# Hash attention before two MLPs: the head outputs' halves moved by DMA and added by GpSimd, the hash products spread over four tiles, and one place in a pair's tiles for every side job

## The chip, the cores and the metric

The kernel runs on one core of a Trainium2 chip. The metric is the device time of one launch in microseconds (us); for the kernel before it is the median of three runs. TensorE, VectorE, ScalarE, GpSimd and SyncE appear in the profile as PE (PEld: its weight loads), DVE, ACT, POOL and SP (SPq: the queue from which SyncE issues DMAs).

## The reference

Inputs q, k and v have the shape (2, 8, 768, 64) in float32; the weights of the MLPs are 64-bit floats.

```
q_bits = einsum('bhsd,dk->bhsk', q, proj) > 0          # 6 bits; k likewise
mask   = q_bucket[:, :, :, None] == k_bucket[:, :, None, :]
scores = where(mask, (q @ k^T) / sqrt(64), -1e9); scores -= max(scores)
attn   = exp(scores); attn = attn / (sum(attn) + 1e-9)
x      = (attn @ v), heads side by side -> (1536, 512)
x      = (silu(x @ w_gate) * (x @ w_val)) @ w_out       # 512 -> 1536 -> 512
out    = layernorm(h * softmax(h)) @ w_out2,  h = x @ w_in2   # 512 -> 1024 -> 512
```

## The kernel before, in words

Every float32 product is made of three products of a faster 32-bit type: a value is cut into a high and a low part, and high x high, high x low and low x high are summed in PSUM.

The attention works on eight **pairs** of heads (pair 0 to 7; 0 to 3 are batch 0). A pair has twelve **tiles** (0 to 11), each of 128 queries of one head against all 768 keys; three tiles make a **quarter** (384 queries of one head), and from pair 1 on the quarters alternate between the two heads, so that both heads' same queries are two quarters in a row, a **half** of the pair. The loop at L722 goes over the 96 tiles and writes all engines' work out by hand (`tc.manual_schedule()`): each engine runs its instructions in exactly the order in which this loop issues them. For tile i an iteration issues the row maxima of tile i (`top`, L491, DVE), the bias and scale made of it (`nm`, L500, DVE), six transposes of the exponentials of tile i-2 (`t`, L531, PE), the scores of tile i+1 (`s`, L480, PE), the high parts (`eh`, L540, ACT) and low parts (`el`, L544, DVE) of the transposes, a third of a quarter's product with v (`av`, L563 and L567, PE), and the exponentials of tile i with their row sums (`e`, L516, ACT). That is the plain work of a tile: on DVE L491, L500 and twice L544.

Beside it run side jobs at fixed tile numbers:
- `split` (L242 and L246, POOL): high and low parts of a later pair's k, q and v, one step a tile (table in `splitting`).
- `turn` (L405, PE; L414 to L424, ACT): six groups of four transposes a pair that turn k and q of a later pair; each is copied out of PSUM by ACT, and DMAs on SP's queue copy rows between partitions (L422, four a head; L425, one a head). The table is `turning`. A turn uses the PSUM bank `pp`, of which there is one.
- `hashes` (L439, PE; L444, DVE): six products of 384 columns in `pp` for each half of the sequence, the bits of which DVE takes out and four small DMAs distribute.
- `sums` and `spread`: 1e-9 is added to a half's row sums (L576, POOL), DVE takes the reciprocal (L578), GpSimd widens it (`wide`, L581, two instructions), three PE transposes bring it to `pp` (L596).
- `results`: a finished `av` holds 64 rows of the product with v's high part and 64 rows of that with its low part. ACT copies the lower 64 rows (`low`, L613), DVE adds them to the upper 64 (L615), once a quarter; once a half DVE multiplies by the spread reciprocals (`xf`, L621), and GpSimd cuts the result into `xh` (L630) and `xl` (L634).
- `early`: twelve DVE steps (L47 to L64) that convert the first 64-bit MLP weights (`w1f`), one after each fourth tile from tile 3 of pair 0 to tile 3 of pair 4 (a DMA takes one of the thirteen places).

`behind` makes a GpSimd instruction wait for the last `nm` that was issued, so that it starts after it. Behind the attention the two MLPs follow; their code is not changed.

Of the kernel before, what the change touches and what calls it, by code (L numbers as in the profile page):

```python
# [20 lines left out]
P = 128  # L21
# [46 lines left out]
def hash_attention_then_two_mlps(  # L68
# [137 lines left out]
    with at:  # L206
# [217 lines left out]
                nc.scalar.copy(qa[:, 1024 - S:S], t)  # L424
                nc.sync.dma_start(qb[0:D].bitcast(F32), qa[0:D].bitcast(F32))  # L425

        def hashes(p, n):
            if p >= len(pairs):
                return
            if n == 0:  # L430
                bits_of[p] = bt.tile([P, S], R32, tag="bits", name="bits")
            cols = slice(HALF * n, HALF * (n + 1))
            t = ps_p.tile([P, 512], F32, tag="pp", name="pp")[:, :HALF]

            for j in range(2):
# [151 lines left out]
        def spread(h):  # L587


            if not 0 <= h < NQ or not ends(h):  # L590
                return
            p, _, n = quarter(h)
# [7 lines left out]
            rs_of[p, n] = rs[:, :HALF]  # L600

        def results(h):
            if not 0 <= h < NQ:
                return
            p, j, n = quarter(h)
# [1 line left out]
            at = slice(j * D, (j + 1) * D)  # L607
            av = av_of.pop(h)
            if j == 0:
                x_of[p, n] = xs.tile([P, HALF], F32, tag="xf", name="xf", bufs=3)  # L610
            xf = x_of[p, n]
# [4 lines left out]
            if not ends(h):  # L616
                return
            del x_of[p, n]
            if p and h < NQ - 1:
                yield  # L620
            nc.vector.tensor_mul(xf, xf, rs_of.pop((p, n)))  # L621
            if h < NQ - 1:
                yield
            cols = slice(b * S + n * HALF, b * S + (n + 1) * HALF)
            if h == NQ - 1:
                nc.scalar.copy(xh[:, hp, cols], xf)
                nc.vector.tensor_sub(xl[:, hp, cols], xf, xh[:, hp, cols].bitcast(F32))
                return
            xh3, xf3 = (x.rearrange("p (c d) -> p c d", d=D) for x in (xh[:, hp, cols], xf))
# [3 lines left out]
            yield  # L633
            behind(nc.gpsimd.tensor_sub(xl[:, hp, cols], xf, xh[:, hp, cols].bitcast(F32)))  # L634

        def go(work):

            next(work, None)

        def turning(p, l):  # L640

            at = {
                0: lambda: turn(p + 1, 0, 1),
                1: lambda: turn(p + 1, 0, 2),
                2: lambda: turn(p + 1, 1, 0),
                3: lambda: turn(p + 1, 1, 1),
                6: lambda: turn(p + 1, 1, 2),
                7: lambda: hashes(p + 1, 0),
                8: lambda: hashes(p + 1, 1),
                9: lambda: turn(p + 2, 0, 0),  # L650
            }
            if p == 1:

                at = {
                    0: lambda: turn(p + 1, 0, 2),
                    2: lambda: turn(p + 1, 1, 0),
                    3: lambda: turn(p + 1, 1, 1),
                    6: lambda: turn(p + 1, 1, 2),
                    7: lambda: hashes(p + 1, 0),
                    8: lambda: hashes(p + 1, 1),  # L660
                    9: lambda: turn(p + 2, 0, 0),
                }
            return at[l]() if l in at else iter(())

        def beginning(i):
# [6 lines left out]
                8: lambda: (hashes(1, 0),),  # L672
                9: lambda: (hashes(1, 1),),
                10: lambda: (turn(2, 0, 0),),
                11: lambda: (turn(2, 0, 1),),
            }
# [19 lines left out]
        def splitting(p, l):  # L696


            if l == 1:
                load(p + 2, "k")  # L700
                load(p + 2, "q")
                load(p + 1, "v")
# [11 lines left out]
        with tc.manual_schedule():  # L714
# [2 lines left out]
            first_weights = early()  # L717
            go(first_weights)
            hashed = start()
            done = summing = leaving = iter(())  # L720
            splits = {}
            for i in range(NSLOT + 9):  # L722
                p, l = divmod(i, SLOTS)
# [5 lines left out]
                if part == 0:  # L729
                    leaving, done = done, results(h - 1)  # L730
                    go(done)
                elif part == 1:
                    go(done)
                maxima(i)
                if part == 0:
                    go(done)
                biases(i)
                transposes(i - 2, 0)
# [8 lines left out]
                for g in range(2):  # L747
                    highs(i - 2, g)
                    lows(i - 2, g)
                if part == 2:  # L750
                    spread(h)
                values(h, part)
                go(work)
                if i == 2:
                    go(hashed)
                if part == 2:
                    go(summing)
# [384 lines left out]
```

## Time and profile before

| | us |
|---|---|
| median of three runs (lowest, highest) | 720.02 (717.36, 720.5) |
| the profiled execution | 719.0 |
| its span, first to last instruction | 717.2 |
| PE busy | 696.4 |
| DVE busy | 567.3 |
| ACT busy | 346.3 |
| POOL busy | 138.3 |

The busy times are sums over the whole span, in which the attention and the MLPs have different limits; they are to be read stage by stage. A matmul's duration includes its way through the array, so PE can be called busy while it is not at its peak.

### The profile page before, as it was taken

To read this page: it belongs to the slowest core of one execution; us is meant where nothing else is said; L and a number is where in the kernel's file an instruction comes from. 1 tells how busy PE (TensorE), PEld (TensorE's weight loads), DVE (VectorE), ACT (ScalarE), POOL (GpSimd) and SP (SyncE) were. 2 spreads that over 40 slices of the span, in tenths; PEclk is the share of its full clock that TensorE was granted. 3 is DMA by queue.
4 is the path that set the end of the run, shared out by engine and by line. 5 is a ranking of instruction groups with operands and counts; after the bars stand their busy time and mean duration, and the time that the engine had idled before them with its cause. 6 is when DMAs were issued, how large, how long until landed. Compare 5 with 4: busy or idle time off the path is not lost.

```text
span 717.2 us, 9973 instructions
## 1 busy us (share of the span) xinstructions
PE 696.4 (97%) x3683; PEld 589.7 (82%) x3683; DVE 567.3 (79%) x988; ACT 346.3 (48%) x676; POOL 138.3 (19%) x157
## 2 busy tenths in 40 slices
PE   8889999999999999999999999999999999999997
PEld 5778898988898887888888888888888888888886
DVE  6899899999889998876797796887987976646461
ACT  6878888888988983343212213122133432222222
POOL 7354345455552314000000000000000000000000
PEclk9999999999999999999999999999999999999999
DMA  6642345260723302322122132232131000000001
GB/s 205 159 116 70 99 121 137 53 165 20 178 60 81 127 1 60 115 85 94 59 75 102 58 118 75 101 90 86 60 118 58 1 0 31 16 29 16 30 15 45
DMA packets 32576, 56.15 MB, mean 78 GB/s; under 512 B 4264, under 2 KB 22952, under 8 KB 32016
## 3 DMA queue, kind: packets, MB, share of 16 engines
q1 hardware_dynamic: 32528, 55.52, 26.5%
q8 instruction: 29, 0.48, 0.3%
q14 instruction: 19, 0.16, 0.1%
HBM read 36.71 MB, written 3.15 MB: 56 GB/s over the span
## 4 chain that ended last, share of the span: by engine, by line
PE 80%; DVE 6%; ACT 5%; DMA 3%; issue 2%; POOL 2%; SPq 0%; ACTq 0%; POOLq 0%
PE h L909 27%; PE h L1022 9%; PE s L480 6%; PE y L935 5%; PE y L934 5%; PE y L936 5%; PE t L531 4%; PE av L563 3%; PE o L1073 3%; PE o L1075 3%; DMA qb<-qa 3%; PE o L1074 3%; PE av L567 2%; ACT eh L540 2%; DVE el L544 2%
## 5 line engine op out<-in xcount | busy, mean ns | idle before, releaser
L909 PE MATMUL h<-xh,lo 128*128 128x512 f32 x288 | 112.3, 390 | 1.1 <-POOL lo L814 1.1
L909 PE MATMUL h<-xh,hi 128*128 128x512 f32 x288 | 112.2, 390 | 0.4 <-ACT hi L813 0.4
L909 PE MATMUL h<-xl,hi 128*128 128x512 f32 x288 | 112.0, 389 | 0.0
L544 DVE TENSOR_TENSOR el<-t,eh 128x384 fp32r<-128x384 f32 x192 | 97.6, 549 | 8.5 <-ACT eh L540 7.7
L516 ACT ACTIVATE e<-s,nm 128x768 f32<-128x768 f32 x96 | 96.8, 1008 | 5.6 <-DVE nm L500 3.0
L491 DVE TENSOR_REDUCE top<-s 128x1 f32<-128x768 f32 x96 | 90.7, 945 | 2.0 <-PE s L480 2.0
L540 ACT CAST eh<-t 128x384 fp32r<-128x384 f32 x192 | 83.6, 487 | 16.7 <-PE t L531 14.9
L1048 POOL TENSOR_TENSOR w<-w,half 128x1 f32<-128x1 f32 x12 | 6.6, 551 | 416.0 <-DVE w L1047 310.8
L531 PE MATMUL t<-idr,e 128*128 128x128 f32 x576 | 81.1, 276 | 0.9 <-DVE el L544 0.7
L531 PEld LDWEIGHTS t<-idr,e 128*128 128x128 f32 x576 | 68.4, 141 | 10.8 <-DVE el L544 4.3
L563 PE MATMUL av<-eh,vs 128*128 128x384 f32 x192 | 67.7, 352 | 0.7 <-DVE xf L615 0.5
L909 PEld LDWEIGHTS h<-xh,lo 128*128 128x128 f32 x288 | 54.1, 188 | 13.1 <-POOL lo L814 1.9
L909 PEld LDWEIGHTS h<-xh,hi 128*128 128x128 f32 x288 | 54.1, 188 | 11.9 <-ACT hi L813 0.7
L909 PEld LDWEIGHTS h<-xl,hi 128*128 128x128 f32 x288 | 54.1, 188 | 11.1
L920 ACT CAST ah<-sg 128x512 fp32r<-128x512 f32 x36 | 22.4, 622 | 75.1 <-DVE sg L918 75.1
L935 PE MATMUL y<-al,hi 128*128 128x512 f32 x144 | 56.0, 389 | 0.0
L936 PE MATMUL y<-ah,lo 128*128 128x512 f32 x144 | 56.0, 389 | 0.0
L934 PE MATMUL y<-ah,hi 128*128 128x512 f32 x144 | 56.0, 389 | 0.0
L480 PE MATMUL s<-ka,qa 128*128 128x384 f32 x192 | 55.9, 372 | 0.0
L918 DVE TENSOR_TENSOR sg<-h,sg 128x512 f32<-128x512 f32 x36 | 24.8, 690 | 38.2 <-PE h L909 23.0
L567 PE MATMUL av<-el,vs 128*64 128x384 f32 x160 | 54.3, 339 | 0.0
L885 ACT CAST hi<-wf 128x1024 fp32r<-128x1024 f32 x17 | 17.9, 1051 | 69.8 <-DVE wf L64 69.8
(191 smaller groups left out, 1419.9 us busy)
## 6 DMA issues: line engine op xcount, KB each, us to landing
raw<-in_moe_w_out_dram SPq DMA_DIRECT2D x10, 1024.0 KB
raw<-in_moe_w_gate_dram SPq DMA_DIRECT2D x12, 512.0 KB
raw<-in_moe_w_val_dram SPq DMA_DIRECT2D x12, 512.0 KB
ka<-kt SPq DMA_DIRECT2D x30, 192.0 KB
raw<-in_moe_w_in_dram SPq DMA_DIRECT2D x4, 1024.0 KB
v<-in_v_dram SPq DMA_DIRECT2D x8, 384.0 KB
kb<-kt SPq DMA_DIRECT2D x15, 192.0 KB
qb<-qa SPq DMA_DIRECT2D x15, 192.0 KB
```

What stands on the lines that cost most here:

```text
L480: nc.tensor.matmul(s[:, n, :HALF], a[:, rows], m[:, n * HALF:(n + 1) * HALF], start=first, stop=not first,)
L491: nc.vector.tensor_reduce(top[:, 1:2], s_of[i][:, :, :HALF], AX.XY, ALU.max, negate=True)
L516: nc.scalar.activation(e, s_of.pop(i)[:, :, :HALF], AF.Exp, bias=nm[:, 1:2], scale=nm[:, 0:1], accum_out=total_of[p, n][:, j, c:c + 1],)
L531: nc.tensor.transpose(t[:, m, :], e_of[i][:, g, m * P:(m + 1) * P], idf)
L540: nc.scalar.copy(half_tile(eh_of, i, g), t_of[i, g])
L544: last_of[i] = nc.vector.tensor_sub(half_tile(el_of, i, g), t_of.pop((i, g)), half_tile(eh_of, i, g).bitcast(F32),)
L563: nc.tensor.matmul(av, vj[:, c], eh_of[h][:, c, :], start=c == 0, stop=c == C - 1)
L567: nc.tensor.matmul(*low, start=False, stop=False)
L909: nc.tensor.matmul(p, a[:, n, kk, :], x[:, kk, blk * BLK:(blk + 1) * BLK], start=kk == 0 and a is hi and x is xh, stop=kk == KD - 1 and a ...
L934: nc.tensor.matmul(p, hi[:, cols], ah, start=f == t * FT, stop=False)
L935: nc.tensor.matmul(p, hi[:, cols], al, start=False, stop=False)
L936: nc.tensor.matmul(p, lo[:, cols], ah, start=False, stop=f == (t + 1) * FT - 1)
```

## The change

`results` no longer adds on DVE. ACT copies all 128 rows of a finished `av` at once, DMAs on SP's queue bring the halves to the other partitions (one for the first head of a half, two for the second), and one GpSimd instruction a half adds them (L645). The last two quarters keep the old way. The 1e-9 is added by DVE instead of GpSimd. `widen`, add, `spread`, multiplication and the cut into `xh` and `xl` follow each other in fixed tiles after the copy. The hashes of pairs 3 to 7 are made with three products a tile in tiles 4 to 7 of the pair before, instead of six in tiles 7 and 8; those of pairs 1 and 2 keep six a tile. Turns, splits, loads and the weight steps get new tile numbers.

```
-        def hashes(p, n):
+        def hashes(p, n, apart=True):
...
             for j in range(2):
+                if j and apart:
+                    yield
+                    yield
...
-            nc.gpsimd.tensor_scalar_add(total, total, 1e-9)
-            yield
+            nc.vector.tensor_scalar_add(total, total, 1e-9)
             nc.vector.reciprocal(r.rearrange("p j c -> p (j c)"), total)
+            r_of[p, n] = r
+
+        def widen(p, n):
+            r = r_of[p, n]
             wide = xs.tile([P, CH, 2, D], F32, tag="wide", name="wide", bufs=1)
...
         def results(h):
...
-            low = xs.tile([D, HALF], F32, tag="low", name="low")
-            nc.scalar.copy(low, av[D:P])
-            yield
-            nc.vector.tensor_add(xf[at], av[0:D], low)
...
+            if j == 0:
+                nc.scalar.copy(xf, av)
+                nc.sync.dma_start(low[0:D], xf[D:P])
+                return
+            both_of = xs.tile([P, HALF], F32, tag="both", name="both", bufs=1)
+            nc.scalar.copy(both_of, av)
+            nc.sync.dma_start(low[D:P], both_of[D:P])
+            nc.sync.dma_start(xf[D:P], both_of[0:D])
+            del x_of[p, n]
+            yield
+            widen(p, n)
+            yield
+            behind(nc.gpsimd.tensor_add(xf, xf, low))
+            yield
+            spread(p, n)
+            yield
+            nc.vector.tensor_mul(xf, xf, rs_of.pop((p, n)))
+            yield
             xh3, xf3 = (x.rearrange("p (c d) -> p c d", d=D) for x in (xh[:, hp, cols], xf))
             behind(nc.gpsimd.tensor_mul(
...
-            yield
             behind(nc.gpsimd.tensor_sub(xl[:, hp, cols], xf, xh[:, hp, cols].bitcast(F32)))
...
         def turning(p, l):
...
+            else:
+                if l in (4, 6):
+                    hashing[:] = [hashes(p + 1, l // 6)]
+                at = {
+                    0: lambda: turn(p + 1, 1, 0),
+                    1: lambda: turn(p + 1, 1, 1),
+                    3: lambda: turn(p + 1, 1, 2),
+                }
+                at.update({n: lambda: hashing[0] for n in range(4, 8)})
+            at.update({
+                9: lambda: turn(p + 2, 0, 0),
+                10: lambda: turn(p + 2, 0, 1),
+                11: lambda: turn(p + 2, 0, 2),
+            })
...
         def splitting(p, l):
-            at = {4: "k", 5: "k", 6: "v", 10: "q", 11: "q", 0: "v"}
+            loads = {6: ((p + 3, "k"),), 9: ((p + 3, "q"),), 0: ((p + 1, "v"),)}
+            at = {2: "k", 4: "k", 5: "q", 8: "q", 10: "v", 11: "v"}
             if p == 0:
-                at = {7: "k", 8: "k", 9: "q", 10: "q", 11: "v"}
...
+                at = {6: "k", 7: "k", 8: "q", 9: "q", 10: "v", 11: "v"}
...
-                if i % 4 == 3:
+                if l in (3, 9, 11):
                     go(first_weights)
```

In the changed kernel a half's `av` is copied in tile 5 (or 11); `widen` follows in tile 6 (0), the add in 7 (1), `spread` and the multiplication in 8 (2), `xh` and `xl` in 9 (3).

DVE's order in tiles 5, 6 and 7 of pair 5. Before (L615 is the add of a quarter, L621 the multiplication, L444 the bits):

```order
L491 TENSOR_REDUCE top_161<-s 128x1
L615 TENSOR_TENSOR xf<-av,low 64x384
L500 SCALAR_TENSOR_TENSOR nm<-top_161 128x2
L544 TENSOR_TENSOR el<-t,eh 128x3x128 x2
L621 TENSOR_TENSOR xf<-xf,pp 128x384
L491 TENSOR_REDUCE top_159<-s 128x1
L500 SCALAR_TENSOR_TENSOR nm<-top_159 128x2
L544 TENSOR_TENSOR el<-t,eh 128x3x128 x2
L491 TENSOR_REDUCE top_160<-s 128x1
L500 SCALAR_TENSOR_TENSOR nm<-top_160 128x2
L544 TENSOR_TENSOR el<-t,eh 128x3x128 x2
L444 TENSOR_SCALAR bits<-pp,over,weigh 128x384
```

The same three tiles of the changed kernel (plain work L495, L504 and L548; bits L448; sums L580 and L581), on DVE:

```order
L495 TENSOR_REDUCE top_161<-s 128x1
L504 SCALAR_TENSOR_TENSOR nm<-top_161 128x2
L548 TENSOR_TENSOR el<-t,eh 128x3x128 x2
L448 TENSOR_SCALAR bits<-pp,over,weigh 128x384
L495 TENSOR_REDUCE top_159<-s 128x1
L504 SCALAR_TENSOR_TENSOR nm<-top_159 128x2
L548 TENSOR_TENSOR el<-t,eh 128x3x128 x2
L580 TENSOR_SCALAR total<-total 128x6
L581 RECIPROCAL r<-total 128x6
L495 TENSOR_REDUCE top_160<-s 128x1
L504 SCALAR_TENSOR_TENSOR nm<-top_160 128x2
L548 TENSOR_TENSOR el<-t,eh 128x3x128 x2
```

L615 is gone from between maximum and bias, the multiplication stands two to three tiles later, and bits and sums have a tile of their own.

GpSimd's order in the changed kernel from tile 0 to tile 9 of pair 5 (L589 `widen`, L645 the new add, L652 and L655 the cut, L242 and L246 the splits):

```order
L589 TENSOR_TENSOR wide<-one,r 128x3x64 x2
L645 TENSOR_TENSOR xf<-xf,low 128x384
L242 TENSOR_TENSOR ks<-k,one 128x12x64
L652 TENSOR_TENSOR xh<-xf,one 128x384
L655 TENSOR_TENSOR xl<-xf,xh 128x384
L246 TENSOR_TENSOR ks<-k,ks 128x12x64
L242 TENSOR_TENSOR qs<-q,one 128x12x64
L589 TENSOR_TENSOR wide<-one,r 128x3x64 x2
L645 TENSOR_TENSOR xf<-xf,low 128x384
L246 TENSOR_TENSOR qs<-q,qs 128x12x64
L652 TENSOR_TENSOR xh<-xf,one 128x384
L655 TENSOR_TENSOR xl<-xf,xh 128x384
```

Each tile has one job of GpSimd; only tiles 3 and 9 have two instructions of the long kind, L652 and L655, one behind the other (before, `xh` and `xl` stood in two different tiles).

SP's queue in the changed kernel, tiles 8 to 1 of pairs 4 and 5 (L635 is the first head's move of a half, L639 and L640 the second's):

```order
L635 DMA low<-xf 64x384
L231 DMA q<-in_q_dram 128x2x384
L422 DMA qb<-kt 64x768
L422 DMA ka<-kt 64x768 x2
L422 DMA kb<-kt 64x768
L639 DMA low<-both 64x384
L640 DMA xf<-both 64x384
L425 DMA qb<-qa 64x768
L231 DMA v<-in_v_dram 128x2x384
```

The two moves of tile 11 stand right behind the four of the turn of tile 10.

## Rows read from the trace of the kernel before

**Rows 1.** Windows: pairs 0 to 7, then an MLP stretch.
```profile
core 0: us, PE busy (x) PEld busy (x) DVE busy (x) ACT busy (x) POOL busy (x), PEclk, DMA share, GB/s
11.12:46.17 35.05, 29.87 (x195) 25.43 (x194) 30.91 (x56) 26.23 (x58) 18.64 (x14) 1.00 0.51 125
46.17:80.61 34.44, 31.37 (x216) 28.40 (x214) 32.32 (x64) 28.29 (x62) 15.95 (x16) 1.00 0.38 96
80.61:114.05 33.44, 32.02 (x210) 29.36 (x210) 30.08 (x61) 27.57 (x60) 16.04 (x16) 0.95 0.44 116
114.05:146.31 32.26, 30.78 (x210) 28.06 (x210) 30.26 (x63) 27.35 (x60) 16.33 (x16) 1.00 0.40 103
146.31:177.17 30.86, 30.56 (x210) 28.04 (x210) 28.74 (x60) 26.62 (x59) 15.34 (x16) 1.00 0.42 108
177.17:208.47 31.30, 30.80 (x213) 28.09 (x210) 28.31 (x59) 27.25 (x61) 16.01 (x17) 1.00 0.44 107
208.47:239.42 30.95, 30.55 (x210) 27.75 (x207) 28.32 (x59) 26.75 (x60) 10.08 (x13) 1.00 0.35 82
239.42:266.30 26.88, 26.12 (x172) 22.66 (x170) 26.24 (x58) 24.48 (x52) 7.92 (x11) 1.00 0.23 80
...
281.30:500.00 218.70, 218.70 (x966) 181.17 (x965) 171.22 (x223) 59.10 (x88) 0.00 (x0) 1.00 0.28 92
```

**Rows 2.** Windows: single tiles (columns as above); the third holds three tiles.
```profile
247.79:249.78 1.99, 1.99 (x16) 1.91 (x15) 1.96 (x6) 1.78 (x5) 0.31 (x1) 1.00 0.86 338
202.89:205.31 2.42, 2.42 (x19) 2.27 (x18) 2.05 (x5) 2.33 (x5) 1.14 (x1) 1.00 0.27 46
181.66:188.91 7.25, 7.25 (x53) 6.74 (x52) 6.47 (x14) 7.20 (x17) 3.80 (x5) 1.00 0.98 258
174.01:177.17 3.16, 3.16 (x24) 2.78 (x22) 2.97 (x7) 2.92 (x8) 1.49 (x2) 1.00 0.00 0
141.81:146.31 4.50, 3.39 (x24) 2.78 (x22) 4.31 (x9) 3.66 (x9) 2.15 (x2) 1.00 0.02 4
```

**Rows 3.** Groups, pairs 0 to 7: count | busy us, mean ns | idle us <-releaser.
```profile
L615 DVE TENSOR_TENSOR xf<-av,low 64x384 f32<-64x384 f32 x30 | 16.4, 548 | 5.4 <-ACT low L613 5.1
L444 DVE TENSOR_SCALAR bits<-pp,over,weigh 128x384 fp32r<-128x384 f32 x14 | 9.4, 668 | 2.7 <-PE pp L439 2.7
L621 DVE TENSOR_TENSOR xf<-xf,pp 128x384 f32<-128x384 f32 x15 | 8.2, 545 | 0.1
...
L581 POOL TENSOR_TENSOR wide<-one,r 128x192 f32<-128x192 f32 x30 | 15.0, 522 | 27.8 <-DVE r L578 27.8
L634 POOL TENSOR_TENSOR xl<-xf,xh 128x384 fp32r<-128x384 f32 x14 | 14.2, 1015 | 18.7 <-DVE nm L500 17.7 <-DVE el L544 1.1
L630 POOL TENSOR_TENSOR xh<-xf,one 128x384 fp32r<-128x384 f32 x14 | 11.6, 827 | 9.6 <-DVE nm L500 9.6
```

**Rows 4.** Timeline, pair 3, tiles 3, 11: start us, us, instruction [idle before <-releaser].
```profile
123.09 0.42 DVE L53 TENSOR_SCALAR w1f<-w1f 128x512 int32<-128x512 int32 x1
...
143.81 1.83 POOL L246 TENSOR_TENSOR qs<-q,qs 128x768 fp32r<-128x768 f32 x1 [1.67 <-DVE nm L500]
144.51 1.41 DVE L62 TENSOR_SCALAR raw<-raw 128x512 int32<-128x512 uint32 x1
146.44 0.36 PE L405 MATMUL pp<-idr,ks 128*128 128x128 f32 x2 [1.24 <-DVE xf L621]
```

**Rows 5.** Timeline: tile 11 of pair 0.
```profile
43.29 1.13 DVE L500 SCALAR_TENSOR_TENSOR nm<-top 128x2 f32<-128x2 f32 x1
44.46 0.36 PE L405 MATMUL pp<-idr,qs 128*128 128x128 f32 x2 [1.68 <-POOL qs L246]
```

**Rows 6.** Timeline: the start of the first MLP.
```profile
271.41 0.50 PE L909 MATMUL h<-xh,lo 128*128 128x512 f32 x1 [1.12 <-POOL lo L814]
```

**Rows 7.** Timeline: a move of pair 0 and the product that waits for it.
```profile
30.21 0.85 SPq L425 DMA_DIRECT2D qb<-qa  x1
34.67 0.41 PE L439 MATMUL pp<-qb,hash_low 128*128 128x384 f32 x1 [1.99 <-DMA qb<-qa]
```

More of the change, by code (lines that the diff above doesn't have):

```diff
@@ L585, in sums, with spread @@
             r_of[p, n] = wide
[L587 to L592, printed above, removed]
+        def spread(p, n):
             wide = r_of.pop((p, n))
@@ L609, in results @@
             if j == 0:
-                x_of[p, n] = xs.tile([P, HALF], F32, tag="xf", name="xf", bufs=3)
-            xf = x_of[p, n]
-            low = xs.tile([D, HALF], F32, tag="low", name="low")
-            nc.scalar.copy(low, av[D:P])
-            yield
-            nc.vector.tensor_add(xf[at], av[0:D], low)
[L616 to L619, printed above, removed]
-                yield
-            nc.vector.tensor_mul(xf, xf, rs_of.pop((p, n)))
-            if h < NQ - 1:
-                yield
-            cols = slice(b * S + n * HALF, b * S + (n + 1) * HALF)
-            if h == NQ - 1:
+                x_of[p, n] = [
+                    xs.tile([P, HALF], F32, tag=tag, name=tag, bufs=bufs)
+                    for tag, bufs in (("xf", 3), ("low", 2))
+                ]
+            xf, low = x_of[p, n]
+            cols = slice(b * S + n * HALF, b * S + (n + 1) * HALF)
+            if h >= NQ - 2:
+                nc.scalar.copy(low[0:D], av[D:P])
+                yield
+                nc.vector.tensor_add(xf[at], av[0:D], low[0:D])
+                if j == 0:
+                    return
+                nc.vector.tensor_mul(xf, xf, rs_of.pop((p, n)))
                 nc.scalar.copy(xh[:, hp, cols], xf)
@@ L628, in results @@
                 return
+            if j == 0:
+                nc.scalar.copy(xf, av)
+                nc.sync.dma_start(low[0:D], xf[D:P])
+                return
+            both_of = xs.tile([P, HALF], F32, tag="both", name="both", bufs=1)
[10 more added lines that the diff above has]
+            yield
+            nc.vector.tensor_mul(xf, xf, rs_of.pop((p, n)))
+            yield
             xh3, xf3 = (x.rearrange("p (c d) -> p c d", d=D) for x in (xh[:, hp, cols], xf))
@@ L638, in go @@
             next(work, None)
+        hashing = []
         def turning(p, l):
[L642 to L651, printed above, removed]
             if p == 1:
@@ L655, in turning @@
                     0: lambda: turn(p + 1, 0, 2),
[L656 to L661, printed above, removed]
-                }
+                    1: lambda: turn(p + 1, 1, 0),
+                    2: lambda: turn(p + 1, 1, 1),
+                    3: lambda: turn(p + 1, 1, 2),
+                    6: lambda: hashes(p + 1, 0, False),
+                    7: lambda: hashes(p + 1, 1, False),
+                }
+            else:
[4 more added lines that the diff above has]
+                    1: lambda: turn(p + 1, 1, 1),
+                    3: lambda: turn(p + 1, 1, 2),
+                }
[5 more added lines that the diff above has]
+            })
             return at[l]() if l in at else iter(())
@@ L671, in beginning @@
                 6: lambda: (turn(1, 1, 2),),
-                8: lambda: (hashes(1, 0),),
-                9: lambda: (hashes(1, 1),),
+                8: lambda: (hashes(1, 0, False),),
+                9: lambda: (hashes(1, 1, False),),
                 10: lambda: (turn(2, 0, 0),),
@@ L696, in splitting @@
         def splitting(p, l):
[L699 to L702, printed above, removed]
-            at = {4: "k", 5: "k", 6: "v", 10: "q", 11: "q", 0: "v"}
-            if p == 0:
-                at = {7: "k", 8: "k", 9: "q", 10: "q", 11: "v"}
+            loads = {6: ((p + 3, "k"),), 9: ((p + 3, "q"),), 0: ((p + 1, "v"),)}
+            at = {2: "k", 4: "k", 5: "q", 8: "q", 10: "v", 11: "v"}
+            if p == 0:
+                loads = {
+                    1: ((p + 2, "k"), (p + 2, "q"), (p + 1, "v")),
+                    8: ((p + 3, "k"),), 10: ((p + 3, "q"),),
+                }
+                at = {6: "k", 7: "k", 8: "q", 9: "q", 10: "v", 11: "v"}
+            for of in loads.get(l, ()):
+                load(*of)
             nm = at.get(l)
@@ L719, in hash_attention_then_two_mlps @@
             hashed = start()
-            done = summing = leaving = iter(())
+            done = leaving = iter(())
             splits = {}
@@ L731, in hash_attention_then_two_mlps @@
                     go(done)
-                elif part == 1:
-                    go(done)
                 maxima(i)
-                if part == 0:
+                if part == 0 and h - 1 >= NQ - 2:
                     go(done)
@@ L749, in hash_attention_then_two_mlps @@
                     lows(i - 2, g)
-                if part == 2:
-                    spread(h)
+                if part == 0:
+                    go(leaving)
+                if part == 2 and h == NQ - 1:
+                    spread(*quarter(h)[::2])
                 values(h, part)
@@ L755, in hash_attention_then_two_mlps @@
                     go(hashed)
-                if part == 2:
-                    go(summing)
                 exps(i)
@@ L762, in hash_attention_then_two_mlps @@
                 splitting(p, l)
-                if part != 2:
-                    go(leaving)
+                go(done if part == 2 else leaving)
+                if part == 0 and h == NQ - 1:
+                    widen(*quarter(h)[::2])
                 if part == 1:
-                    summing = sums(h + 1)
-                    go(summing)
-                if i % 4 == 3:
+                    go(done)
+                    sums(h + 1)
+                if l in (3, 9, 11):
                     go(first_weights)
```

1 line of the change is left out of this document (removed).

## The prediction

> **What bounds the kernel now.** I read the windows first, one for each pair of heads, from the start of its first maximum to that of the next pair's [rows 1]. In the MLP stretch PE is busy for 218.70 of 218.70 us and nothing that the change touches runs there, so whatever it gives or takes lies in the 255.2 us of the eight pairs and in the seam behind them. The pairs are unequal: 30.86 to 31.30 us for pairs 4 to 6, 32.26 to 34.44 for 1 to 3, 35.05 for pair 0, 26.88 for pair 7, which turns nothing. In none of them is one engine full: PE shows 30.8 of 31.30 in pair 5, DVE 28.3, ACT 27.3.
>
> So I went down to tiles [rows 2]. A plain tile takes 1.99 us and fills PE (1.99) and DVE (1.96) alike; ACT has 1.78 to do. A tile with one turn takes 2.42: PE is full, DVE has 2.05, so a turn costs PE 0.43 (0.108 a transpose) and DVE waits meanwhile. In three tiles with two turns and one result copy ACT is busy for 7.20 of 7.25 us: its plain 3 x 1.78 = 5.34 and 1.86 of copies; there ACT sets the pace. The tile with an add and a multiplication on DVE takes 3.16, where DVE has 2.97. Each side job thus lengthens the tile in which it stands on whichever engine it loads, the others idle, and the next tile gives little back. The question for every part is what falls into the same tile.
>
> A product of 384 columns comes out of the plain tile: (1.99 - 6 x 0.108) / 8 = 0.17 us. A pair's PE work is then 12 x 1.99 + 6 turns x 0.43 + 12 hash products x 0.17 + two spreads x 0.32 = 29.1 us. Pair 5 takes 31.30, so 2.2 us at most are to be had in such a pair.
>
> The fourth view is the timeline of the slow tile 11 of pair 3 [rows 4]. It takes 4.50 us where the same tile in pair 4, without a weight step, takes 3.16 [rows 2]. The weight step L62 starts at 144.51 while GpSimd is in a split until 145.64, and ends at 145.92: 1.41 us, most of it waiting for GpSimd to finish. The multiplication L621 comes after it, and PE, which needs the bank pp, idles 1.24 us. The step L53 of tile 3, where GpSimd was nearly through, took 0.42. The bias of a tile can be caught too: in tile 11 of pair 0, where GpSimd was late with the split of q and PE waited 1.68 us for it, L500 took 1.13 us [rows 5].
>
> **The change part by part.**
>
> *The add leaves DVE.* Thirty L615 of 0.548 go [rows 3]; what that is worth depends on the tile, and is counted in the tile prices below. ACT's copy grows from 64 to 128 rows of the same length; I cost that at nothing, since ACT's own casts have 128 rows and no longer length per column; if it were dearer it would show in the tiles where ACT is full. The new GpSimd add is priced as L634, 1.02 us, 14 times; GpSimd has 16 of 31 us to do in a pair [rows 1], so it is hidden as long as its operands are there.
>
> *The side jobs move apart.* By the same prices the new tiles of a pair need: on PE 2.42 in the six turn tiles, 1.99 + 3 x 0.17 = 2.50 in the four hash tiles, 2.31 in the two spread tiles. On DVE the multiplication makes 1.99 + 0.5 = 2.5 in tiles 2 and 8; the bits 2.6 in 5 and 7 [rows 3]; the sums, two tiny instructions that must outwait widen (2 x 0.52 from the bias on, while the two el take 1.02), between 2.2 and 2.8 in tiles 0 and 6, of which I take 2.6. So DVE exceeds PE by 0.1 to 0.2 in six tiles, 0.6 together if nothing is smoothed. ACT has all six turns and three copies in the eight tiles from 8 to 3: 8 x 1.78 + 3 x 1.86 = 19.8, against PE's 8 x 1.99 + 6 x 0.43 + 2 x 0.32 = 19.1: 0.7 more. A pair so lies between 29.1 (PE alone) and 30.4 (no smoothing); since the ACT-paced tiles of before show none, I take 30.2. The small waits of PE for the turned q before the hashes go, because turn and hash are now two tiles apart; they are within this sum.
>
> *The weight steps.* Twelve in all; after the change nine fall into pairs 1 to 4 (3, 2, 3, 1) and all into tiles 3, 9 and 11. There GpSimd starts on its tile's job just after the bias and is in it for 0.83 + 1.02 (xh and xl) or 1.83 us (v), and the step comes 1.0 to 1.4 us after the bias. Before, one step in three met that, now all do, which speaks against the change. Cost of one: at most 4.50 - 3.16 = 1.34 [rows 2]; at least 0, as for L53. In a turn tile DVE has 0.43 to spare and the next tile gives some back; I take 1.34 - 0.43 - 0.3 = 0.6.
>
> The Trainium skill says this as a rule (SBUF — State Buffer, section "SBUF: two separate sides"): GpSimd and those DVE instructions that use its second port exclude each other for a whole instruction. The trace agrees in L62 and L500; taken strictly, every one of the nine steps pays the whole wait, and the sum below would be smaller by 9 x 0.7 = 6.3 us.
>
> *The sum by pair,* before and after:
> - Pair 0, 35.05 to 34.05: PE's wait of 1.68 for the split of q goes, as that split ends two tiles earlier [rows 5], and with it L500's wait at the same time; the weight steps in tiles 9 and 11 take back 0.7. PE's 1.99 us for the move of the turned q in tile 8 stays [rows 7]: nothing of it is changed.
> - Pair 1, 34.44 to 33.4: 30.2, a seventh turn 0.4, three steps 1.8, and about 1.0 where two GpSimd jobs meet in a tile (k's split and an add in tile 4, xl and widen in tile 6, as this pair gets its halves later) and hold the next bias, by L500's 1.13.
> - Pair 2, 33.44 to 31.4: 30.2 + 1.2. Its granted clock is 0.95 now, that is, some 3 us at 1.2 instead of 2.4 GHz after the longest stall of PE; that stall goes.
> - Pair 3, 32.26 to 32.0: 30.2 + 1.8. Pair 4, 30.86 to 30.8: 30.2 + 0.6. Pair 5, 31.30 to 30.2.
> - Pair 6, 30.95 to 28.6: no turn in tiles 9, 10, 11 (0.4 + 0.5 + 0.7 off 30.2).
> - Pair 7, 26.88 to 25.9: 12 x 1.99 + 2 x 0.5 (multiplications) + 2 x 0.5 (sums).
> - Seam: PE waits 1.12 for GpSimd's lo [rows 6]; now eight products of av stand between, 1.4 us, though two widen instructions precede lo on GpSimd. Between 0 and 1.12, I take 0.7.
>
> The gains are 1.0 + 1.0 + 2.0 + 0.3 + 0.1 + 1.1 + 2.3 + 1.0 + 0.7 = 9.5 us. The profiled execution took 719.0 (span 717.2), the median of the three runs is 720.02; 719.0 - 9.5 = 709.5 and 720.0 - 9.5 = 710.5. I say 710.
>
> **The rivals.**
>
> *The weight steps are hidden.* If DVE gets its turn between xh and xl, or PE's lead of a tile covers the wait, they cost what L53 cost, nothing on the path: 5.4 us more gain in pairs 1 to 4, about 704. For it: two PSUM tiles each of s and t let PE run ahead. Against it: tile 11 now, where nothing was covered. Chance 0.15.
>
> *GpSimd's lock takes the gain.* Each step pays 1.34 and the pairs come to 30.4: the sum falls by 9 x 0.7 + 7 x 0.2 = 7.7 to 1.8 us, about 717.5. For it: L62 and L500; against it: DVE has 0.43 to spare in every turn tile, which it had not in tile 11 of before. It is the Trainium skill's rule above taken at its word. Chance 0.16.
>
> *The moves come late: slower.* The add in tile 1 needs the two moves of tile 11, which stand behind four of 192 KB on SP's queue. From the copy's end to the add there are two tiles, some 4.8 us. The move L425 of pair 0, itself behind nine others, was issued at 30.21 and waited for until 34.67: 4.5 us [rows 7]. If the new ones take over 4.8, GpSimd waits; beyond about 5.8 the multiplication in tile 2 stops DVE, then PE by pp, and every further us counts once a half, 14 times: one us makes 709.5 + 14 = 723.5. Against it: at tile 5 the queue is empty, and at tile 11 two halves of such a move are queued behind four, not nine. Chance 0.09.
>
> **How the numbers follow.** The forecast has 0.60. Its own range is 705 to 714: the weight steps between 0.2 and 1.0 each, a pair between 29.8 and 30.4. For 8 in 10 the range must reach most of the hidden steps and of the lock: 703 to 718, which leaves out the late moves and the far ends of both, 0.17. A measurement of this kernel can tell about 0.5% (3.6 us) from no change. Faster by more, under 716.4: the forecast nearly whole, the hidden steps, and a third of the lock, 0.79; within it 0.12; slower 0.09.
>
> **What would show it.** Right: tiles without weight steps near 2.4 to 2.6, pairs 5 near 30.2 with PE without gaps; L615 seen twice only; weight steps in tiles 3, 9 and 11 of about 1.0 to 1.4 us, ending 0.3 after GpSimd; no PE wait for qs in pair 0. Wrong: GpSimd's add ending idle time behind a DMA, DVE's multiplication waiting for it, PE waiting for pp; or pair 5 above 31, which would mean that ACT or the sums in tiles 0 and 6 hold more than I allow.

## The result and the profile after

The changed kernel takes 702.91 us, the median of four runs (702.44 to 704.01), beside 720.26 (717.36 to 721.93) for the kernel before on the same chip: a ratio of 0.977 [0.973, 0.980], some 17 us less. The median lies 0.1 us under the low end of the range of 703 to 718, the profiled execution, 704.01 with a span of 702.2, inside it; the forecast of 710 was some 7 us too high. PE's share of the chain that ended last is 93% (80% before).

The windows of the profile after, cut as those of before [rows 1]: pairs 0 to 7, then an MLP stretch of 219 us.

```profile
core 0: us, PE busy (x) PEld busy (x) DVE busy (x) ACT busy (x) POOL busy (x), PEclk, DMA share, GB/s
11.86:47.64 35.78, 33.56 (x200) 28.82 (x199) 30.34 (x55) 25.82 (x60) 18.70 (x12) 0.86 0.55 140
47.64:77.86 30.22, 30.22 (x220) 28.78 (x218) 28.90 (x61) 27.17 (x64) 17.58 (x16) 1.00 0.59 153
77.86:107.52 29.66, 29.66 (x211) 27.89 (x209) 27.98 (x59) 26.24 (x61) 17.70 (x16) 1.00 0.59 149
107.52:137.44 29.92, 29.92 (x216) 28.47 (x215) 28.67 (x61) 26.72 (x63) 18.10 (x16) 1.00 0.53 132
137.44:166.33 28.89, 28.89 (x203) 27.16 (x202) 27.38 (x58) 25.54 (x59) 17.50 (x16) 1.00 0.52 129
166.33:196.03 29.70, 29.70 (x212) 28.26 (x210) 27.52 (x58) 26.35 (x61) 17.58 (x17) 1.00 0.45 106
196.03:225.03 29.00, 29.00 (x201) 27.33 (x199) 27.02 (x57) 25.41 (x57) 10.21 (x13) 1.00 0.40 97
225.03:251.97 26.94, 26.91 (x181) 23.96 (x179) 25.75 (x57) 24.80 (x56) 9.81 (x13) 1.00 0.34 106
281.00:500.00 219.00, 219.00 (x968) 181.39 (x967) 171.52 (x225) 56.75 (x84) 0.00 (x0) 1.00 0.26 87
```

The MLP stretch is full of PE as before. In pairs 1 to 6 PE is now busy for the whole window, where before it missed 0.3 to 3.1 us. Beside the forecast:

| pair | before | forecast | after | weight steps |
|---|---|---|---|---|
| 0 | 35.05 | 34.05 | 35.78 (34.18 in a repeat) | 3 |
| 1 | 34.44 | 33.4 | 30.22 | 3 |
| 2 | 33.44 | 31.4 | 29.66 | 2 |
| 3 | 32.26 | 32.0 | 29.92 | 3 |
| 4 | 30.86 | 30.8 | 28.89 | 1 |
| 5 | 31.30 | 30.2 | 29.70 | 0 |
| 6 | 30.95 | 28.6 | 29.00 | 0 |
| 7 | 26.88 | 25.9 | 26.94 | 0 |
| sum | 255.18 | 246.35 | 240.11 | |

The pairs give 15.1 us and what follows them 0.7 (702.2 - 251.97 = 450.2, before 717.2 - 266.30 = 450.9); the start takes 0.7 more (first maximum at 11.86 instead of 11.12). That is the 15.0 us between the two profiled executions.

PE's waits in the attention, before: for DVE's multiplication at `pp`, for the moved q, for GpSimd's split of q, and one in tile 2 of pair 1 that is put down to a bias, where the multiplication, which reads `pp` too, had ended 0.14 us earlier.

```profile
PE pp L405 <- DVE xf L621: 4.0, 3, 1.5
PE pp L439 <- DMA qb<-qa: 3.4, 7, 2.0
PE pp L405 <- POOL qs L246: 2.1, 3, 1.7
PE pp L405 <- DVE nm L500: 1.2, 1, 1.2
PE t L531 <- DVE el L544: 0.7, 3, 0.3
```

After (us in total, times, longest):

```profile
engine line waited for: us in total, times, longest us
PE av L567 <- DVE xf L626: 1.4, 1, 1.4
PE pp L355 <- DVE qb L379: 0.9, 1, 0.9
PE pp L443 <- DMA qb<-qa: 0.5, 1, 0.5
PE pp L405 <- DVE bits L364: 0.4, 1, 0.4
PE t L535 <- DVE el L548: 0.3, 1, 0.3
```

The first row belongs to the last quarters, which keep the old way; the other four belong to pair 0 and the start. In pairs 1 to 6 PE waits for nothing.

By the windows, pairs 1 to 7 became 15.8 us shorter. Half of that, 7.9 us, is time in which PE was idle before. The other half lies in PE's busy time, which fell from 212.2 to 204.3 us, 1.7 of it at most by the clock of pair 2. Stops of PE can hide there: products that follow each other every 0.17 us are recorded with 0.33 to 0.34 us each, so a shorter stop leaves no gap. That the other half went the way of the waits is therefore likely and not shown.

The weight steps are the place where the forecast went furthest off. DVE and GpSimd in the timeline, first a step in tile 9 of pair 1, then one in tile 11 of pair 3 (L548 is `el`, L504 the bias):

```profile
71.14 0.83 POOL L652 TENSOR_TENSOR xh<-xf,one 128x384 fp32r<-128x384 f32 x1 [0.67 <-DVE nm L504]
71.91 0.42 DVE L62 TENSOR_SCALAR raw<-raw 128x512 int32<-128x512 uint32 x1
72.05 1.15 POOL L655 TENSOR_TENSOR xl<-xf,xh 128x384 fp32r<-128x384 f32 x1
...
135.39 1.84 POOL L246 TENSOR_TENSOR vs<-v,vs 128x768 fp32r<-128x768 f32 x1 [0.52 <-DVE nm L504]
135.47 1.02 DVE L548 TENSOR_TENSOR el<-t,eh 128x384 fp32r<-128x384 f32 x2 [0.22 <-ACT eh L544]
136.41 1.11 DVE L62 TENSOR_SCALAR raw<-raw 128x512 int32<-128x512 uint32 x1
```

The same line L62 takes 0.42 us where GpSimd is at the seam of its two instructions, and it is L655 that is stretched; under one long split it takes 1.11 and ends 0.29 after the split. Six of the nine steps in pairs 1 to 4 stand in tiles 3 and 9 and do not wait (0.42 to 0.68 us, by their kind): five at such a seam, and that of tile 3 of pair 1 beside an idle GpSimd. The three in tile 11 wait (0.85 to 1.11 us).

What the waiting ones cost is read from tiles. Windows of tile 11 without a step (pair 4) and with one (pair 3), of tile 9 with a step (pair 3), and of tile 2 of pair 5:

```profile
163.67:166.33 2.66, 2.66 (x21) 2.54 (x20) 2.05 (x5) 2.66 (x7) 1.90 (x2) 1.00 0.65 143
134.10:137.44 3.34, 3.34 (x29) 3.19 (x28) 3.08 (x7) 3.34 (x9) 2.61 (x2) 1.00 0.78 168
129.51:132.11 2.60, 2.60 (x23) 2.49 (x21) 2.57 (x7) 2.23 (x5) 1.84 (x3) 1.00 0.35 71
170.93:174.05 3.12, 3.12 (x24) 2.89 (x23) 2.97 (x7) 3.05 (x7) 2.39 (x2) 1.00 0.84 202
```

Tile 11 is 0.68 us longer with a step, but the tile 2 that comes behind it is shorter: 2.57 in pair 3, behind a tile 11 with a step, and 3.12 in pair 5, behind one without. It looks as if ACT, which is busy for the whole of either tile 11 (3.34 of 3.34 and 2.66 of 2.66), used the time that DVE takes and had less to catch up on. Over whole pairs three steps cost 29.92 - 29.70 = 0.2 us.

The last piece is the move. SP's queue and GpSimd around the end of pair 4, where it is latest:

```profile
163.95 1.23 SPq L422 DMA_DIRECT2D ka<-kt  x2
165.56 0.47 SPq L422 DMA_DIRECT2D kb<-kt  x1
166.14 0.64 SPq L639 DMA_DIRECT2D low<-both  x1
166.88 0.69 SPq L640 DMA_DIRECT2D xf<-both  x1
...
171.51 1.00 POOL L645 TENSOR_TENSOR xf<-xf,low 128x384 f32<-128x384 f32 x1 [2.92 <-DVE el L548]
171.91 0.62 DVE L504 SCALAR_TENSOR_TENSOR nm<-top 128x2 f32<-128x2 f32 x1
```

The add starts 4.6 us after its second move was issued, in tile 2 instead of tile 1, and catches the bias L504 there (0.62 instead of 0.16). The copy of `av` had ended at 164.98; SP's queue was still issuing the turn's four, so that the second move was issued 1.9 us after the copy. Ten of the 15 adds (the prediction counted 14) start 1.4 to 1.5 us after GpSimd's idle time began and wait for no transfer; three wait for one: this one, that of tile 1 in pair 2, and the last.

### The profile page after: what moved, and what is told of

Its sections match the earlier page's. It is cut to its first block, busy times and chain, and to the rows that moved or that the text cites. A ratio compares the mean times of both kernels' runs of the same rounds, so it can differ in the third digit from the quotient of the medians.

```text
span 702.2 us, 10083 instructions
## 1 busy us (share of the span) xinstructions
PE 692.0 (99%) x3683; PEld 592.8 (84%) x3683; DVE 557.0 (79%) x974; ACT 339.3 (48%) x676; POOL 150.6 (21%) x156
## 4 chain that ended last, share of the span: by engine, by line
PE 93%; DVE 2%; issue 2%; ACT 2%; DMA 1%; POOL 0%; SPq 0%; ACTq 0%; POOLq 0%; DVEq 0%
PE h L937 28%; PE h L1050 10%; PE s L484 9%; PE t L535 8%; PE y L963 5%; PE y L964 5%; PE y L962 5%; PE av L567 4%; PE av L571 4%; PE o L1101 3%; PE o L1103 3%; PE o L1102 3%; PE pp L443 2%; PE pp L405 2%; PE t L1088 1%
## 5 line engine op out<-in xcount | busy, mean ns | idle before, releaser
L548 DVE TENSOR_TENSOR el<-t,eh 128x384 fp32r<-128x384 f32 x192 | 97.8, 550 | 9.2 <-ACT eh L544 6.8
L495 DVE TENSOR_REDUCE top<-s 128x1 f32<-128x768 f32 x96 | 90.6, 944 | 3.7 <-PE s L484 3.5
L567 PE MATMUL av<-eh,vs 128*128 128x384 f32 x192 | 66.2, 345 | 1.4 <-DVE xf L626 1.4
```

Of the source, the lines that this page charges most:

```text
L495: nc.vector.tensor_reduce(top[:, 1:2], s_of[i][:, :, :HALF], AX.XY, ALU.max, negate=True)
L548: last_of[i] = nc.vector.tensor_sub(half_tile(el_of, i, g), t_of.pop((i, g)), half_tile(eh_of, i, g).bitcast(F32),)
L567: nc.tensor.matmul(av, vj[:, c], eh_of[h][:, c, :], start=c == 0, stop=c == C - 1)
```

## The experiments

Each kernel was timed beside the kernel before, whose median was 719.63 us beside the first four, 720.15 beside the next four and 720.46 beside the last four. "Pairs 1 to 7" is the sum of their windows, 204.33 in the changed kernel (204.35 in its repeat) and 220.13 before; it leaves out pair 0, which varies from one execution to the next.

**The changed kernel again.**

> The changed kernel once more. The profiled execution of it had 35.8 us in pair 0, with 5.03 us in its tile 1, where the kernel before had 35.05 and 2.98. If that start is an accident of one execution, this profile shows tile 1 of pair 0 near 3 us, pair 0 near 34 and a span of 700 to 701; if the change lengthens the start, it shows about 5 us there again. Time 702 to 704 either way.

703.01 us (701.82 to 704.20), ratio 0.977 [0.975, 0.979]. The window of pair 0 in it:

```profile
11.12:45.30 34.18, 30.23 (x200) 25.91 (x199) 28.95 (x55) 25.85 (x60) 19.41 (x12) 1.00 0.59 150
```

PE's 200 instructions take 30.23 us here at a granted clock of 1.00, and 33.56 in the first profile at 0.86 (a mean; where it was low is shown in the last section). Tile 1 takes 2.98 us and the span is 699.9, so the changed kernel does not always start as slowly as in the first profile. Pair 0 is thus known to some 1.6 us only.

**The moves alone.** The new `results`, `widen` and `spread`, with the 1e-9 on DVE, in the kernel before; turns, hashes, splits, loads and weight steps keep their old tile numbers.

```
-            nc.vector.tensor_add(xf[at], av[0:D], low)
+                nc.sync.dma_start(low[0:D], xf[D:P])
...
+            behind(nc.gpsimd.tensor_add(xf, xf, low))
```

> The kernel before with the new way of the head outputs alone (one ACT copy, moves by DMA, GpSimd's add, widen, spread and multiplication in fixed tiles, 1e-9 on DVE); turns, hashes, splits, loads and weight steps stand in the tiles of before. Theory A, the add that left DVE is worth most: 708 or less. Theory B, the places are worth most: 714 or more, with xh and xl and the splits meeting in GpSimd's tiles and the turns and hashes where they were.

720.14 us (717.86 to 722.50), ratio 1.000 [0.998, 1.002]; pairs 1 to 7 take 222.02. Thirty adds have left DVE, and nothing is gained. PE's waits in the attention of this kernel, and then the window of tile 8 of pair 5:

```profile
PE pp L443 <- DMA qb<-qa: 3.5, 7, 1.2
PE pp L600 <- DVE bits L448: 2.8, 6, 1.2
PE t L535 <- DVE el L548: 2.8, 7, 0.6
PE pp L600 <- ACT kt L414: 1.7, 5, 0.4
```

```profile
199.20:203.68 4.48, 4.16 (x28) 3.69 (x27) 3.19 (x6) 2.23 (x5) 0.00 (x0) 1.00 0.12 26
```

Before, PE waited for a multiplication at `pp`; now `spread` (L600) waits for bits and for turns at the same bank, and the hashes wait for q as before. Tile 8 has hashes, bits, spread and multiplication and takes 4.48 us, of which DVE works 3.19.

**The places alone.** The changed kernel with the add back on DVE, twice a half, between maximum and bias, and no moves.

```
+            nc.scalar.copy(low[0:D], av[D:P])
+            yield
+            nc.vector.tensor_add(xf[at], av[0:D], low[0:D])
...
-            behind(nc.gpsimd.tensor_add(xf, xf, low))
```

> The changed kernel with the add back on DVE (ACT copies 64 rows, DVE adds 64 rows in each quarter between maximum and bias; no moves, no GpSimd add), all places as in the changed kernel. Theory A (add on DVE is dear, as each tile lasts as long as its fullest engine): DVE then has 3.0 us in tiles 2 and 8 and 3.1 in tile 5, some 0.5 each more than now, 10 us over seven pairs: 712 to 714. Theory B (PE is the pace of a pair and runs ahead over DVE's full tiles): 703 to 706.

711.17 us (709.43 to 712.19), ratio 0.988 [0.985, 0.990]; pairs 1 to 7: 211.27. The time lies just under theory A's range and far from theory B's. The places alone give some 8.5 us, the moves alone nothing, both together 17: the two parts are not a sum. By pairs, the moves add on top of the places 1.66, 1.23, 1.11 and 0.89 us in pairs 1 to 4, which have weight steps, 0.29 and 0.60 in pairs 5 and 6, and 1.15 in pair 7.

**The hashes joined again,** six products in each of tiles 6 and 7.

```
-                at.update({n: lambda: hashing[0] for n in range(4, 8)})
+                at.update({
+                    6: lambda: hashes(p + 1, 0, False),
+                    7: lambda: hashes(p + 1, 1, False),
+                })
```

> The changed kernel with the hash products of pairs 3 to 7 joined again, six products in tile 6 and six in tile 7. By tile prices PE has 3.0 us in tiles 6 and 7 and 1.99 in 4 and 5, the same sum as four tiles of 2.5: 702 to 704. If the split of the products is what lets PE run without gaps (bank pp, bits on DVE), 0.5 us or more a pair are lost: 705.5 or more.

703.77 us (703.11 to 704.17), ratio 0.978 [0.976, 0.980]; pair 5 takes 29.64. Tiles 4 and 5 shrink to 2.1 and tiles 6 to 8 grow to 2.9 to 3.0. That the hashes are cut into threes is worth nothing here.

**The weight steps in their old tiles,** 3, 7 and 11.

```
-                if l in (3, 9, 11):
+                if i % 4 == 3:
```

> The changed kernel with the weight steps at their old tiles 3, 7 and 11. Theory A of the prediction (a step costs 0.6 us wherever GpSimd is in a long job): tile 7 has GpSimd's add of 1.0 us and the bits instead of tile 9's two instructions; 702 to 705. If the new tiles were what hid the steps: 707 or more.

703.79 us (702.98 to 704.42), ratio 0.977 [0.976, 0.979]. The steps in tile 7 of pairs 1 to 3 take 0.42 to 0.68 us, without a wait. No difference that can be told.

**The weight steps under a long split,** in tiles 4, 8 and 11.

```
-                if l in (3, 9, 11):
+                if l in (4, 8, 11):
```

> The changed kernel with the weight steps in tiles 4, 8 and 11, where GpSimd is in one instruction of 1.83 us, instead of 3, 9 and 11, where in two of the three it is in two instructions of 0.8 and 1.0. Theory A (between two GpSimd instructions DVE gets its turn, within one it waits for the end): the steps in tiles 4 and 8 take 0.8 to 1.1 us as those of tile 11 do, each costs 0.5 to 0.7, 3 to 5 us in all: 706 to 708. Theory B (PE's lead covers a step wherever it stands): 702 to 704.

704.91 us (703.87 to 706.42), ratio 0.979 [0.977, 0.981]; pairs 1 to 7: 207.16. In pairs 1 to 4 every step now waits (among them L53 1.19, L57 1.22 and 1.29, L64 1.25 and 1.49 us). Three of the nine wait in the changed kernel too, so it is six more waits that cost these pairs 2.8 us, 0.5 each: 1.35 in pair 1, where GpSimd's add follows k's split in tile 4, and 1.5 for the other four. The time lies between the two theories, and the price of a step in tiles 4 and 8 is near theory A's.

**The second head's moves issued twice.**

```
+            for _ in range(2):
+                nc.sync.dma_start(low[D:P], both_of[D:P])
+                nc.sync.dma_start(xf[D:P], both_of[0:D])
```

> The changed kernel with both moves of a half's second head issued twice (same data to the same place), so that the add waits for about one us more of transfers. If the moves have time to spare: 702 to 704, nothing in the tiles. If they are at their limit already, the add is late by 1 us in the half of tile 11, the bias or the multiplication of tile 2 waits, seven times: 707 to 711.

710.01 us (709.90 to 710.25), ratio 0.986 [0.984, 0.987]; pairs 1 to 7: 209.13. GpSimd's adds in tile 1 are late; that of pair 5 comes 2.2 us into tile 2 (which begins at 172.78), and that tile takes 3.76 us. GpSimd's waits for the move (four, the longest 4.6 us, 13.6 together), and the one of pair 5 in the timeline:

```profile
POOL xf L646 <- DMA xf<-both: 13.6, 4, 4.6
```

```profile
175.02 1.01 POOL L646 TENSOR_TENSOR xf<-xf,low 128x384 f32<-128x384 f32 x1 [4.58 <-DMA xf<-both]
```

The moves of the changed kernel have little time to spare: two more transfers of 96 KB in a half are paid, with 4.8 us in pairs 1 to 7 and 2.3 behind them, where the last add starts 5.8 instead of 3.5 us after the last maximum.

**A third of the hash products left out** (the low ones, from pair 1 on; 28 products, by 0.17 us 4.8 us of PE).

```
+                    if m < 2:
```

> The changed kernel without the hash products of the queries' low parts (hash_low) for pairs 1 to 7: two products of three; this part of the computation is left out. PE loses 7 x 4 products of 0.17 us, 4.8 us. Theory A (PE alone paces the pairs now): 698 to 699. Theory B of the prediction (ACT's copies and DVE's full tiles set 30.2 a pair): 701 or more.

699.18 us (699.11 to 699.39), ratio 0.971 [0.969, 0.972]: 3.7 of 4.8 us come back, nearer to theory A. In pairs 2 to 6 it is 3.05 of 3.4 (20 products): there PE's work now counts almost in full.

**The third weight step in tile 1 instead of 11.**

```
-                if l in (3, 9, 11):
+                if l in (3, 9, 1 if p else 11):
```

> The changed kernel with the weight step of tile 11 moved to tile 1 from pair 1 on (tile 1 of a pair has one GpSimd instruction, the add, which ends before the step comes). Theory A, each step under the 1.83-us split in tile 11 costs what it waits, about 0.7 us in each of pairs 1 to 3 (tile 11 takes 3.33 to 3.62 with a step and 2.67 without): 3 x 0.7 = 2.1 us less, about 701. Theory B, the wait falls into time in which ScalarE is behind anyway (pair 5, with no step at all, takes 29.67, pair 3, with three, 29.96; tile 2 takes 2.5 to 2.6 in pairs with a step and 3.13 to 3.18 in pairs 5 and 6 without): tile 11 shortens to about 2.7 and tile 2 grows by as much, 702.5 to 703.5.

707.51 us (704.70 to 708.92), ratio 0.982 [0.979, 0.985]. Slower, by a cause that neither theory had; the row is from tile 3 of pair 2:

```profile
90.84 0.43 DVE L47 TENSOR_SCALAR w1f<-raw 128x512 int32<-128x512 int32 x1 [3.67 <-DMA raw<-in_moe_w_val_dram]
```

The new place also brings the later steps forward. The load of the second weights, issued at 84.19 in tile 1 of pair 2, now stands two tiles ahead of the step that needs it; in the changed kernel it is issued at 86.97 in tile 3, six tiles ahead. Two tiles are too short for it, and pair 2 takes 34.45. Of the theories, the second fits the rest: pair 1 is 1.0 shorter (29.22 instead of 30.22), but the tile 2 behind its tile 11 takes 3.12 instead of 2.52, and pairs 3 and 4, which the load does not touch, take 59.38 together instead of 58.81.

**The 1e-9 on GpSimd again.**

```
-            nc.vector.tensor_scalar_add(total, total, 1e-9)
+            nc.gpsimd.tensor_scalar_add(total, total, 1e-9)
```

> The changed kernel with the 1e-9 added by GpSimd again, at the old distance of an instruction. DVE's L580 leaves tiles 0 and 6 (0.16 to 0.59 us each), but the reciprocal now waits for GpSimd. Theory A, GpSimd is free there and DVE's share of that tile is the price: 0.2 to 0.3 us in 14 tiles less if DVE paced them, up to 3 us, 700 to 703. Theory B, the tile is not paced by DVE, or DVE waits for GpSimd's answer as long as it did for its own: no difference, 703 to 704. Theory C, the reciprocal stops DVE behind GpSimd's queue: 0.5 to 1.0 in each of 14 tiles, 710 to 717.

706.69 us (703.94 to 707.05), ratio 0.981 [0.978, 0.984]; pairs 1 to 7: 207.05. Between theories B and C: DVE waits 8.2 us in 14 reciprocals, longest in tile 6 of pair 1, where `xl` and another `widen` stand ahead of L580 on GpSimd:

```profile
61.86 0.97 POOL L589 TENSOR_TENSOR wide<-one,r 128x192 f32<-128x192 f32 x2
62.92 0.24 POOL L580 TENSOR_SCALAR total<-total 128x6 f32<-128x6 f32 x1
63.19 0.19 DVE L581 RECIPROCAL r<-total 128x6 f32<-128x6 f32 x1 [1.77 <-POOL total L580]
```

Pair 1 grows by 1.1 us, pairs 2, 3, 4 and 6 by 0.3 each, pair 5 not at all, pair 7 by 0.5.

**The hashes in tiles 7 and 8,** six products each, beside spread and multiplication.

```
+                at.update({n: lambda n=n: hashes(p + 1, n - 7, False) for n in (7, 8)})
```

> The changed kernel with the hashes of pairs 3 to 7 six products a tile in tiles 7 and 8, the places they had before; tile 8 then holds hash, bits, spread and multiplication on the one bank pp, as in the kernel that had only the moves (tile 8 took 3.98 to 4.48 us there, 2.57 in the changed kernel, and tiles 4 to 7 would give back what the hashes leave there). Theory A, sharing pp in tile 8 is what kept the moves from paying: tile 8 grows by 1.4 to 1.9, tiles 4 to 7 shrink by 0.5 to 1.0 together, 0.5 to 1.4 in each of five pairs, 706 to 710. Theory B, the collision is hidden by TensorE's lead: 703 to 704.

706.75 us (704.99 to 708.72), ratio 0.982 [0.979, 0.985]; pairs 1 to 7: 206.77, 0.3 to 0.8 more in each of pairs 2 to 6. Tile 8 of pair 5:

```profile
187.73 0.67 DVE L448 TENSOR_SCALAR bits<-pp,over,weigh 128x384 fp32r<-128x384 f32 x1
188.54 0.52 PE L600 MATMUL pp<-idr,wide 128*128 128x128 f32 x3 [0.33 <-POOL qs L246]
189.16 0.55 DVE L649 TENSOR_TENSOR xf<-xf,pp 128x384 f32<-128x384 f32 x1 [0.76 <-POOL qs L246]
```

L600 writes the bank that L448 reads until 188.40, and DVE stands for 0.76 us. The rows here name the split of q, which ended at 188.50; `wide` was made two tiles before, and in three of the five such tiles PE's wait is put down to L448. Theory A at its low end: the tile takes 4.25 us instead of 2.57, of which 1.0 are six products at 0.17 that left tiles 4 to 7; those take 1.4 less together, and the pair 0.45 more.

**Both steps of v's split earlier,** in tiles 6 and 10.

```
-            at = {2: "k", 4: "k", 5: "q", 8: "q", 10: "v", 11: "v"}
+            at = {2: "k", 4: "k", 5: "q", 8: "q", 6: "v", 10: "v"}
```

> The changed kernel with v's two split steps in tiles 6 and 10 instead of 10 and 11. Tile 6 then holds widen and a split step on GpSimd, as tile 0 did in the kernel with the moves alone, where L580 took 1.1 us and the tile 3.24. Theory A, GpSimd's two jobs in one tile are what kept the moves from paying: 0.6 to 0.9 us in each of pairs 1 to 6, less what tile 11 gives back where a weight step stood under the split (three times 0.7 at most): 704 to 708. Theory B, it is covered: 702 to 704.

703.09 us (701.25 to 703.36), ratio 0.976 [0.973, 0.979]; pairs 1 to 7: 203.98. L580 takes 0.78 us in tile 6 of pair 5, under the split, and the tile 2.92 instead of 2.36; tiles 7, 8 and 10 give back 0.23, 0.12 and 0.20, and the pair takes 29.67, as in the repeat. Theory B: a GpSimd collision of that size is covered. In pairs 1 to 4, where no step waits now, the pairs take 118.26 together instead of 118.69. This version cannot be told from the changed kernel, and none here that does the whole work is shown to be faster than that.

## Why the prediction was right, and where it was off

The direction held, and the mechanism as far as the profile shows it: with side jobs in tiles of their own PE's waits are gone, which are half of what pairs 1 to 7 gained. The time came out 7 us lower, outside the forecast's own range of 705 to 714; it fell on the rival in which the weight steps are hidden (704), to which the prediction gave 0.15. By pairs the misses are larger than those 7 us, with both signs: pairs 1 to 4 came 8.9 us under the forecast, pair 5 another 0.5, while pairs 0, 6 and 7 came 1.7, 0.4 and 1.0 over it.

*The weight steps* are the term that was furthest off: "after the change nine fall into pairs 1 to 4", and "I take 1.34 - 0.43 - 0.3 = 0.6", 5.4 us together. They cost 0.2 in pair 3 for three. Two things were missed. I took `xh` and `xl` for one job of 1.85 us; DVE gets in between the two instructions, as that rival had it, so that six of nine do not wait. The three that wait are nearly made good elsewhere: tile 11 grows by 0.68, tile 2 of the next pair shrinks by 0.55. The kernel with the steps in tiles 4, 8 and 11 shows the price where every step waits, 0.5 us for each of the six more. So the price of 0.6 was not far off for a step that waits; how many wait, and what tile 11 gives back, was.

*GpSimd's lock* did not take the gain. The rule of the Trainium skill that the prediction weighed (SBUF — State Buffer, section "SBUF: two separate sides": exclusive for a whole instruction) agrees with the rows shown, 1.11 under the 1.84-us split and 0.42 at a seam; the mistake was to apply it to a job instead of an instruction.

*A pair's base price.* I took 30.2 from between 29.1 and 30.4. Pair 5, which has no step, takes 29.70; in pairs 1 to 4 that half microsecond makes 2.0. The smoothing between tiles is better than I allowed, and the kernel without the low hash products shows how near PE alone is to setting the pace: 3.05 of 3.4 us in pairs 2 to 6.

*Pair 1's collisions,* 1.0: they exist (L580 took 0.59 us in tile 6) and cost about nothing, as the kernel with v's split in tile 6 shows for such a wait. Steps, base and collisions make 5.4 + 2.0 + 1.0 = 8.4 of the 8.9 us.

*Pair 2's clock* is 1.00 instead of 0.95, as said. The stall before it fell was not PE's longest, though: it fell behind a wait of 1.50 us at the start of pair 2 (0.50 from 82 to 85 us), and stayed at 1.00 behind those of 1.99 and 1.68 in pair 0 (35 to 46 us). *The seam* gave 0.7 as said, in part by luck: PE's waits for `lo` (1.12) and for the high part beside it (0.40) are gone, and its wait for the last add grew from 0.50 to 1.42.

*Pair 7* was a slip in reading. Its window [rows 1] ends 3.0 us after the last maximum, because I let it, and the forecast counted that tile with 1.99. With the same end nothing was to be had there. *Pair 6* has tile 2 and tile 5 at 3.12, which I priced at 2.5 and 2.6, and gives two thirds of that back in others. *Pair 0* was to come to 34.05 and took 34.18 in the repeat; in the profile after, two tiles at the lower clock hid it.

*The moves come late* is partly real. GpSimd's add ending idle time behind a DMA was named as a sign of being wrong; it is seen three times. The limit of 4.8 us was counted from the copy's end, and from there to the add it is 6.5 us at the end of pair 4: 1.9 until SP's queue issues the second move, which the estimate left out, and 4.6 from that issue. Even so only the bias is held, by 0.46; the multiplication, which starts 8.6 us after the copy's end, does not wait for it. Two more transfers a half cost 7 us.

*Add and places.* "What that is worth depends on the tile" was right, and more than I wrote: without the new places the add's leaving is worth nothing. ACT's copy of 128 rows was costed right (0.48 us, as the 0.475 of 64 rows before). Of what holds it back there, the hashes beside spread at `pp` are shown (2.4 us in pairs 2 to 6); GpSimd's two jobs in tile 6 (L580 0.78) are not it, by themselves, while the longer collision of that kernel in tile 0 (L580 1.1) was not tried. The waits for q in tile 7 (3.5 us in seven), behind a turn in tile 6, were not tried apart, and how these add up to the whole stays open.

## What to carry to other kernels

Taking work off an engine paid here only once that engine was what the next wait ended on; remove the shared bank and the queue from the tile first, then see what the lighter engine is worth. When no wait is left, price a disturbance over the whole pair, not over its tile: here three steps that lengthen their tiles by 0.34, 0.60 and 0.68 us cost the pair 0.2, while six steps under long GpSimd instructions cost 0.5 each. When a window is compared with a sum, give both the same end.

## What the runs showed of the hardware that was not expected

A DVE instruction of 0.42 us gets through between two GpSimd instructions issued back to back, and GpSimd's second one is the one that is stretched (L655 1.15 us, and 1.42 under the longer L64, instead of 1.00). Even an instruction on 128 x 6 elements waits: L580 takes 0.16 us alone and 0.78 under a split (tile 6 of the last kernel).

The clock at the start differs between executions of the same program. Windows of tile 1 of pair 0, in the first profile and in the repeat:

```profile
15.31:20.34 5.03, 5.03 (x14) 3.38 (x14) 2.23 (x3) 1.21 (x4) 4.87 (x4) 0.50 0.55 159
```

```profile
13.32:16.30 2.98, 2.98 (x14) 2.05 (x14) 2.23 (x2) 0.76 (x3) 2.90 (x3) 1.00 0.82 224
```

In the first, PE had waited 0.48 and 0.54 us at 6.1 and 7.2 us, and the granted clock was 0.50, 1.2 GHz, from 8.4 us or just before until within tile 2; in the repeat these waits were 0.23 and 0.14 (one of 0.17 came at 9.0), and it stayed at 1.00, 2.4 GHz. Tile 1 ends at 20.34 in the one and at 16.30 in the other, pair 0 at 47.64 and 45.30. Ten of the fourteen profiles here take over 4.2 us in that tile. The one profile of the kernel before takes 2.98; whether its other executions start slowly as often is not shown, though they too differ (717.55 us at a mean granted clock of 1.00, 722.80 at 0.99). That is why sums over pairs 1 to 7 tell small changes apart better than the time of one launch.
